# Two layers of Fourier mixing and sliding-window attention: preset far scores, a later weight split, a norm that starts sooner, and a fixed order of the last rows

## The chip, the core and the metric

The kernel runs on one core of a Trainium2 chip. A core has five engines that run their own instruction streams in order: TensorE (PE: matmuls, with weight loads shown apart as PEld), VectorE (DVE), ScalarE (ACT), GpSimd (POOL) and SyncE (SP), which here issues nearly all DMAs. SBUF is the working memory; matmuls write to PSUM, in banks of 512 float32 per partition. The metric is the device time of one execution in microseconds, lower is better. The time before is the median of three runs, 2053.36 us (2048.55 to 2053.51).

## The reference

Four sublayers are applied to one sequence of S = 2048 rows of D = 640: Fourier mixing, attention, Fourier mixing, attention, with the same weights both times.

```python
x = x + _A_ref(_layernorm(x), dft_seq_re, dft_seq_im, dft_hid_re, dft_hid_im)
x = x + _B_ref(_layernorm(x), wqkv, wo)
x = x + _A_ref(_layernorm(x), ...)
x = x + _B_ref(_layernorm(x), wqkv, wo)

def _A_ref(x, ...):          # real part of a two-dimensional DFT
    a, b = x @ hid_re.T, x @ hid_im.T
    return seq_re @ a - seq_im @ b

def _B_ref(x, wqkv, wo):     # H = 32 heads of 20, window W = 256
    q, k, v = split(x @ wqkv)
    scores = q @ k.T * 20 ** -0.5
    mask = (i - j >= 0) & (i - j < W)      # else -1e9
    return softmax(scores) @ v, heads joined, @ wo
```

## The kernel before, in words

Every float32 product is made of three fp16 matmuls: each operand is split into a high half and a remainder (`hi`, `lo`), and hi·hi, hi·lo and lo·hi are summed in PSUM. A split is a ScalarE cast (`hi`) and a subtraction on VectorE or GpSimd (`lo`).

`spectral` is the Fourier sublayer. `attention` is the other one; the change lies in it alone. It walks over steps G = 0 to 127 (`g` = 2G). A step is one tile of 128 query rows (`i`) and four heads; 16 steps make a block `b` of 256 rows (two tiles, eight groups of four heads), and even steps take the first tile of the block, odd ones the second. Block 0 is steps 0 to 15. A query tile sees three key tiles: its own, the one before and, two back, the far one, of which the causal window leaves the part above the diagonal.

In a step stand, on the engines named:

- `scores` (PE): near scores into the PSUM tiles `sq` (`near`), far scores into the first 256 columns of the PSUM tiles `sk` (`farq`). There are two of each, for two pairs of heads, and no second buffer: the next step writes the same tiles.
- `largest` (VectorE): L1175 copies the far scores over the masked triangle of the near ones, and L1177 takes the row maximum into `m`. The first two tiles (`i` < 2, steps 0 to 15) have no far tile; there the copy takes a constant tile `neg` in SBUF, spread over the heads.
- `by_key` and `probabilities` (PE, ScalarE L1231, GpSimd L1235 and L1237), 8 steps later: the scores once more, by key, with the maxima folded in as two more rows of the contraction, through an exponential into `ptq`, and the masks.
- `values` and `back`, 11 steps after the scores: the products with `v` (into `pf`, copied to `pvs` by ScalarE, L1263), two transposes with `idf`, a division on VectorE (`r` L1279, `o` L1280), and the split into `os` on GpSimd (L1282, L1283).
- one unit of filling work for PE (`run_unit`), 15 matmuls: projections of the next block to q and k (`pf<-early,big`, 128x256), to v (`pf<-big,early`, 128x320), or output products (`pf<-bo,ot`, 128x320). A unit is ready when its step has come and what it needs is done, and the one with the smallest due step goes first.
- one to three steps of slow work (`slow_step`): the norm of the rows that a later block projects (`rows_norm`: statistics L139, aggregates, eight small instructions L148 to L152, `lny` L166, and a split whose GpSimd half is `rx` L178), and, when none is left, idle work: in the first layer the split of the output weights.

That split is `split_wo`: five chunks of `wo`, each a load into `wst`, a ScalarE instruction (L1013) and a VectorE instruction (L1014) into `bo`. The first layer alone does it, from step 0 on. Output products need it (`"wo"` in a unit's needs).

The rows of blocks 2 and later are loaded from DRAM and normalised two blocks ahead. Those of block 2 are wanted at step 0, those of block 3 at step 6; a new norm was allowed only 4 `g` after the last had ended, and started 4 `g` behind its load.

At the end of a layer the last two tiles have no later work to hide behind. Their output products are made in three parts, for the 128-column groups 0 to 2, 3 and 4 of `os`, as soon as the last block's head groups give them: PE transposes `os` (`turned`), VectorE copies to `ot` (L1046), and the products are summed in the banks of `sq` and `sk` that are free by then. The three parts were units (`last_out`) in the order of their due steps.

`in_line` and `issue_after` keep the order in which the code is written on an engine; where they are not used, a list scheduler of the framework may place an instruction of VectorE or ScalarE a little earlier or later.

## Time and profile before

| | us |
|---|---|
| median of 3 runs | 2053.36 (2048.55 to 2053.51) |
| profiled execution | 2055.41 |
| its span, first to last instruction | 2053.7 |
| busy in the span: PE, DVE, POOL, ACT | 1986.1, 1568.6, 1475.1, 1112.4 |
| steps 0 to 15, first copy to that of step 16: layer one, layer two | 59.1, 58.4 |
| first copies of the layers | 557.7, 1568.1 |

The first attention starts with the copy at 557.7 us and the second with that at 1568.1 us. A row of the timeline has the start, the duration, the engine, the line, the operation with what it writes and reads, the number of merged instructions, and in brackets how long the engine had idled and for whom. Times of `pf` matmuls with the same operands can be compared with one another. "PEclk" in the windows view is the share of TensorE's clock that was granted in that stretch.

### The profile page before, as it was taken

To read this page: it belongs to the slowest core of one execution; us is meant where nothing else is said; L and a number is where in the kernel's file an instruction comes from. 1 tells how busy PE (TensorE), PEld (TensorE's weight loads), DVE (VectorE), ACT (ScalarE), POOL (GpSimd) and SP (SyncE) were. 2 spreads that over 40 slices of the span, in tenths; PEclk is the share of its full clock that TensorE was granted. 3 is DMA by queue.
4 is the path that set the end of the run, shared out by engine and by line. 5 is a ranking of instruction groups with operands and counts; after the bars stand their busy time and mean duration, and the time that the engine had idled before them with its cause. 6 is when DMAs were issued, how large, how long until landed. Compare 5 with 4: busy or idle time off the path is not lost.

```text
span 2053.7 us, 55762 instructions
## 1 busy us (share of the span) xinstructions
PE 1986.1 (97%) x21881; PEld 1449.5 (71%) x21881; DVE 1568.6 (76%) x3261; ACT 1112.4 (54%) x1959; POOL 1475.1 (72%) x2168
## 2 busy tenths in 40 slices
PE   6999999999989999999999999999999999999998
PEld 4777777776767777777667777777676677777765
DVE  8888778768588888777648778787776788886673
ACT  5544555534247777666644444444332576766665
POOL 5777788877457788776657778777783587777754
PEclk9999999999999999999999999999999999999999
DMA  7556566566544544434645455454744454443232
GB/s 274 178 197 203 174 209 226 179 242 215 148 111 102 126 125 112 105 93 103 166 132 177 153 184 178 151 172 145 284 161 129 88 129 118 120 121 95 72 85 74
DMA packets 280508, 311.10 MB, mean 151 GB/s; under 512 B 107572, under 2 KB 214836, under 8 KB 271156
## 3 DMA queue, kind: packets, MB, share of 16 engines
q1 hardware_dynamic: 279668, 306.88, 50.0%
q8 instruction: 171, 2.80, 0.6%
q14 instruction: 93, 0.76, 0.1%
q10 hardware_dynamic: 576, 0.66, 0.1%
HBM read 201.72 MB, written 83.46 MB: 139 GB/s over the span
## 4 chain that ended last, share of the span: by engine, by line
PE 69%; DVE 14%; issue 5%; POOL 4%; DMA 4%; ACT 3%; SPq 0%; DVEq 0%; POOLq 0%; ACTq 0%
PE pf L126 32%; PE y L126 11%; PE x L126 11%; PE z L126 7%; PE sk L126 5%; DVE cc L558 3%; PE sq L126 3%; DVE sq L1175 2%; DVE m L1177 2%; ACT ptq L1231 2%; DMA res<-accd 2%; DVE lnt L151 1%; POOL cs L548 1%; DVE res L581 1%; DVE lnst L139 1%
## 5 line engine op out<-in xcount | busy, mean ns | idle before, releaser
L126 PEld LDWEIGHTS <-cc 128*128 128x128 f16 x5376 | 524.4, 98 | 213.1 <-issue 13.4
L1231 ACT ACTIVATE ptq<-sk,shift,alpha 128x768 f32<-128x768 f32 (+2 forms) x512 | 472.5, 945 | 122.9 <-PE sk L126 70.7
L126 PEld LDWEIGHTS <-big 128*128 128x128 f16 x4320 | 415.1, 99 | 131.0 <-issue 25.0
L1177 DVE TENSOR_REDUCE m<-sq 128x2 f32<-128x512 f32 (+1 forms) x512 | 345.6, 675 | 19.4 <-POOL os L1282 0.5
L126 PE MATMUL pf<-early,big 128*128 128x256 f16 x2400 | 295.1, 277 | 0.1
L555 ACT ACTIVATE cc<-cs 128x512 f16<-128x512 f32 x256 | 153.7, 625 | 260.3 <-POOL cs L548 149.8
L126 PE MATMUL y<-zc,cc 128*128 128x320 f16 x1728 | 262.8, 299 | 3.2 <-DVE pf L581 3.2
L1235 POOL TENSOR_SCALAR_AFFINE_SELECT ptq<-ptq 128x512 f32<-128x512 f32 x224 | 142.7, 637 | 167.7 <-ACT ptq L1231 165.1
L558 DVE SCALAR_TENSOR_TENSOR cc<-cs,cc 128x512 f16<-128x512 f32 x256 | 248.1, 978 | 7.6 <-ACT cc L555 7.5
L1175 DVE COPY_PREDICATED sq<-mask,sk 128x256 f32<-128x256 int32 x448 | 189.5, 423 | 53.4 <-PE sq L126 51.6
L558 DVE SCALAR_TENSOR_TENSOR cc<-cq,cc 128x512 f16<-128x512 f32 x192 | 205.8, 1073 | 0.1
L126 PE MATMUL pf<-ptq,v 128*32 128x128 f32 (+1 forms) x3840 | 183.6, 329 | 3.1 <-DVE x L956 2.6
L126 PE MATMUL z<-zc,cc 128*128 128x320 f16 x1152 | 177.7, 299 | 5.4 <-DVE res L581 4.4
L1237 POOL TENSOR_SCALAR_AFFINE_SELECT ptq<-ptq 128x512 f32<-128x512 f32 x256 | 166.1, 649 | 19.6 <-ACT ptq L1231 19.4
L126 PE MATMUL x<-zc,cc 128*128 128x320 f16 x1152 | 177.7, 299 | 0.0
L387 ACT ACTIVATE qf<-pf 128x256 f32<-128x256 f32 x160 | 61.2, 383 | 166.1 <-PE pf L126 132.8
L126 PEld LDWEIGHTS pf<-ptq,v 128*32 128x32 f32 x3840 | 110.7, 110 | 45.5 <-DVE x L956 3.9
L126 PE MATMUL pf<-big,early 128*128 128x320 f16 x960 | 141.4, 300 | 0.0
L547 POOL TENSOR_TENSOR cs<-cq 128x512 f32<-128x512 f32 x64 | 86.8, 1357 | 68.3 <-DVE cc L558 67.7
L126 PEld LDWEIGHTS <-qs 62*128 62x128 f16 x2688 | 90.3, 94 | 59.1 <-issue 55.8
L126 PE MATMUL pf<-bo,ot 128*128 128x320 f16 x840 | 123.8, 300 | 0.8 <-DVE x L956 0.8
L126 PE MATMUL x<-big 128*128 128x320 f16 x825 | 122.3, 299 | 2.0 <-DVE big L447 2.0
(144 smaller groups left out, 3484.3 us busy)
## 6 DMA issues: line engine op xcount, KB each, us to landing
cq<-in_cmat_dram SPq DMA_DIRECT2D x64, 1024.0 KB
accd<-res SPq DMA_DIRECT2D x96, 320.0 KB
res<-accd SPq DMA_DIRECT2D x96, 320.0 KB
x<-x2d SPq DMA_DIRECT2D x64, 320.0 KB
qkd<-early SPq DMA_DIRECT2D x160, 128.0 KB
ks<-qkd SPq DMA_DIRECT2D x108, 160.0 KB
qs<-qkd SPq DMA_DIRECT2D x84, 160.0 KB
x2d<-res SPq DMA_DIRECT2D x32, 320.0 KB
```

The lines of the kernel that those rows point to most:

```text
L126: i = getattr(nc.tensor, what)(*args, **kw)
L139: nc.vector.bn_stats(st[:, h], x[:, h * 320:(h + 1) * 320])
L151: ts(u, g, g, h, op0=OP.mult, op1=OP.mult)
L387: nc.scalar.activation(f, pf[:, :QB], AF.Copy, scale=down)
L547: g.tensor_tensor(s1, a21, a22, op=OP.add)
L555: nc.scalar.activation(cc[m][:, 0], f, AF.Copy, scale=C_UP)
L558: nc.vector.scalar_tensor_tensor(cc[m][:, 1], f, C_UP, cc[m][:, 0], op0=OP.mult, op1=OP.subtract)
L1175: marks["dve"] = nc.vector.copy_predicated(near[pi][:, :, 0], mask[:, None, :].to_broadcast([P, 2, P]), far).ins
L1177: marks["dve"] = nc.vector.tensor_reduce(TOP[n][:, pi, :, k], near[pi][:, :, :1 + (i >= 1)], axis=AX.XY, op=OP.max).ins
L1231: marks["act"] = nc.scalar.activation(o[:, pi], tps[pi][:, :, first:], AF.Sigmoid, bias=shift, scale=alpha[:, 0:1]).ins
L1235: nc.gpsimd.affine_select(out=q[:, :, a0], in_=q[:, :, a0], pattern=[[0, 4], [-1, P]], base=0, channel_multiplier=1, compare_op=OP.is_gt, ...
L1237: ins = nc.gpsimd.affine_select(out=q[:, :, a0 + 2], in_=q[:, :, a0 + 2], pattern=[[0, 4], [1, P]], base=0, channel_multiplier=-1, compare ...
```

## The change

1. Far scores preset: `neg` is gone. At the start of each attention VectorE sets the far columns of both `sk` tiles to NEG, in PSUM, and for `i` < 2 the copy reads them there as it reads far scores later.
2. The weight split is queued at `g` = 34 (step 17, in block 1) in place of step 0, with two slow steps in place of three between chunks. Output tiles of block 0 wait for it, also their load and transposition.
3. Rows of block 3: the next rows' load may be issued as soon as a norm has ended, and the norm starts 8 `g` after the last one's end at the earliest.
4. In the second layer the last two tiles follow one generator, `last_rows`, that goes part by part and tile by tile, and `turn_rows` issues the transposes of a part as soon as its `os` is there. The first layer keeps `last_out`.
5. The last head group's `os` split is on ScalarE and VectorE in place of GpSimd, in both layers, and the second tile's last copy to `ot` in the second layer is on ScalarE.

```diff
+            for f in farq:
+                nc.vector.memset(f, NEG)
...
-                far = farq[pi] if i >= 2 else neg[:, None, :].to_broadcast([P, 2, P])
-                    marks["dve"] = nc.vector.copy_predicated(near[pi][:, :, 0], mask[:, None, :].to_broadcast([P, 2, P]), far).ins
+                    marks["dve"] = nc.vector.copy_predicated(near[pi][:, :, 0], mask[:, None, :].to_broadcast([P, 2, P]), farq[pi]).ins
...
+WO_STEP = 34
-            if layer == 0:
-                idle.append(split_wo())
+                if layer == 0 and g == WO_STEP:
+                    idle.append(split_wo())
-                    for _ in range(3):
+                    for _ in range(2):
-                        need = [(i - 2, 2)] if i > 1 else []
+                        need = [(i - 2, 2)] if i > 1 else ["wo"] * (layer == 0)
...
-            wanted, x2s, normed_at = [], [], [-FREE_STEPS]
+            wanted, x2s, normed_at = [], [], [-2 * FREE_STEPS]
-                if wanted and x2s and g >= x2s[0] + 4 * (g > 0):
+                if wanted and x2s and g >= max(x2s[0] + 4 * (g > 0), normed_at[0] + 2 * FREE_STEPS):
-                if wanted and not slow and not x2s and g >= normed_at[0] + FREE_STEPS:
+                if wanted and not slow and not x2s and g > normed_at[0]:
...
-                nc.gpsimd.tensor_copy(hi, o)
-                nc.gpsimd.tensor_tensor(lo, o, hi, op=OP.subtract)
+                if last and k == NP // 2 - 1:
+                    nc.scalar.activation(hi, o, AF.Copy)
+                    nc.vector.tensor_tensor(lo, o, hi, op=OP.subtract)
+                else:
+                    nc.gpsimd.tensor_copy(hi, o)
+                    nc.gpsimd.tensor_tensor(lo, o, hi, op=OP.subtract)
...
+            def last_rows(tiles):
+                for i in tiles:
+                    while (i - 2, 2) not in done:
+                        yield 0
+                    x3 = keep.tile([P, D], F32, tag="res1", name="x3", bufs=2)
+                    load(x3, x2_d[i])
...
+                for k in range(3):
+                    for i in tiles:
+                        while (i, k) not in turned_at or turned_at[i, k] >= now[0] or i % 2 and now[0] < NG + 2 * KEY_LAG \
+                                or k == 1 and len(parts) < 3:
+                            yield 0
+                        ot, acc, x3 = OT[i]
+                        d0, d1, at = parts[k]
+                        for n in range(2):
+                            yield from out_products(ot, acc[n], n, d0, d1)
...
+            def turn_rows():
+                for k, (d0, d1, at) in enumerate(parts if final else ()):
+                    for i in (S // P - 2, S // P - 1):
+                        if (i, k) not in turned_at and i in OT and at < now[0]:
+                            for _ in turned(i, d0, d1, i % 2 and d1 == ND):
+                                pass
+                            turned_at[i, k] = now[0]
```

How the rows of an engine's stream move is shown at three places, all on VectorE. (Line numbers of the changed kernel are higher: L1175 became L1218, L1177 L1220, L1014 L1050, L166 L165, L1046 L1085, L1279 and L1280 L1322 and L1323.) First, the end of step 1 and step 2 of the first layer's attention; before:

```order
L1175 COPY_PREDICATED sq_6969<-mask,neg 128x256
L1177 TENSOR_REDUCE m<-sq_6969 128x2
L1014 SCALAR_TENSOR_TENSOR bo_67<-wst,wsc,bo_66 128x640
L1175 COPY_PREDICATED sq_6968<-mask,neg 128x256
L1014 SCALAR_TENSOR_TENSOR bo_67<-wst,wsc,bo_66 128x640
L1177 TENSOR_REDUCE m<-sq_6968 128x2
L1175 COPY_PREDICATED sq_6969<-mask,neg 128x256
L1177 TENSOR_REDUCE m<-sq_6969 128x2
L139 BN_STATS lnst<-x_7003 128x6 x2
```

and with the change:

```order
L1218 COPY_PREDICATED sq_6967<-mask,sk_6969 128x256
L1220 TENSOR_REDUCE m<-sq_6967 128x2
L1218 COPY_PREDICATED sq_6966<-mask,sk_6968 128x256
L1220 TENSOR_REDUCE m<-sq_6966 128x2
L1218 COPY_PREDICATED sq_6967<-mask,sk_6969 128x256
L1220 TENSOR_REDUCE m<-sq_6967 128x2
L138 BN_STATS lnst<-x_7003 128x6 x2
```

Both splits of `bo` are gone from between the copies, and the copies read `sk`; the two MEMSETs that fill it stand ahead of the layer's first copy.

Second, the end of the norm of block 2's rows, and the copies of step 6; before:

```order
L166 TENSOR_SCALAR lny<-x_7003,lnmv,lnt 128x640
L152 TENSOR_SCALAR lnt<-lnt 128x1
L151 TENSOR_SCALAR lnt<-lnt 128x1
L152 TENSOR_SCALAR lnt<-lnt 128x1
L166 TENSOR_SCALAR lny<-x_7004,lnmv,lnt 128x640
L1175 COPY_PREDICATED sq_6968<-mask,neg 128x256
L1177 TENSOR_REDUCE m<-sq_6968 128x2
L1175 COPY_PREDICATED sq_6969<-mask,neg 128x256
L1177 TENSOR_REDUCE m<-sq_6969 128x2
```

and with the change:

```order
L165 TENSOR_SCALAR lny<-x_7003,lnmv,lnt 128x640
L151 TENSOR_SCALAR lnt<-lnt 128x1
L150 TENSOR_SCALAR lnt<-lnt 128x1
L151 TENSOR_SCALAR lnt<-lnt 128x1
L1218 COPY_PREDICATED sq_6966<-mask,sk_6968 128x256
L165 TENSOR_SCALAR lny<-x_7004,lnmv,lnt 128x640
L1220 TENSOR_REDUCE m<-sq_6966 128x2
L1218 COPY_PREDICATED sq_6967<-mask,sk_6969 128x256
L1220 TENSOR_REDUCE m<-sq_6967 128x2
```

The first copy of the step now stands ahead of the second `lny`; its maximum still follows that `lny`.

Third, the end of the second layer; before:

```order
L1046 COPY ot<-pf 128x2x384
L1279 RECIPROCAL r<-pf 128x8
L1280 TENSOR_TENSOR o<-pf,r 128x160
L1046 COPY ot<-pf 128x2x384
L1046 COPY ot<-pf 128x2x128
L1279 RECIPROCAL r<-pf 128x8
L1280 TENSOR_TENSOR o<-pf,r 128x160
L1046 COPY ot<-pf 128x2x128 x3
```

and with the change:

```order
L1085 COPY ot<-pf 128x2x384 x2
L1322 RECIPROCAL r<-pf 128x8
L1323 TENSOR_TENSOR o<-pf,r 128x160
L1085 COPY ot<-pf 128x2x128 x2
L1322 RECIPROCAL r<-pf 128x8
L1323 TENSOR_TENSOR o<-pf,r 128x160
L1328 TENSOR_TENSOR os<-o,os 128x2x80
L1085 COPY ot<-pf 128x2x128
```

Both tiles' copies of the first part now stand together, and the copies of the second part lie ahead of the last division; the last split (L1328) is VectorE's, and one copy of the last part has left for ScalarE. On PE the transposes of the first tile's first part now precede the last but one group of key products, the products of the second part follow the last `pvs` transposes, and the last products are the third part's 12 as before.

The five weight splits now stand on VectorE behind the 42nd, 44th, 48th, 68th and 70th copy of the first layer, where they stood behind the 4th, 5th, 20th, 40th and 44th; ScalarE's halves stand correspondingly. In fifteen places of blocks 1 to 4 of the first layer PE's filling unit is another than before, an output product for a projection or the other way, and each is 15 matmuls as before; no other engine but SP has more or fewer instructions than the five points say.

More of the change, by code (lines that the diff above doesn't have):

```diff
@@ L88, in body @@
     mask = pers.tile([P, P], I32, name="mask")
-    neg = pers.tile([P, P], F32, name="neg")
     shift = pers.tile([P, 1], F32, name="shift")
@@ L97, in constants @@
         nc.gpsimd.memset(mask, 1)
-        nc.gpsimd.memset(neg, NEG)
         nc.gpsimd.memset(shift, SHIFT)
@@ L933, in last_out @@
                         yield from next_layer(i, x3)
+            def last_rows(tiles):
[4 more added lines that the diff above has]
+                    load(x3, x2_d[i])
+                    OT[i] = (sb.tile([P, 2, ND, P], F16, tag="ot", name="ot", bufs=2),
+                             [t[:, 4 * P:] for t in kst] if i % 2 else qst, x3)
+                for k in range(3):
[7 more added lines that the diff above has]
+                            yield from out_products(ot, acc[n], n, d0, d1)
+                            if d1 == ND:
+                                cs = slice(n * 320, (n + 1) * 320)
+                                nc.vector.scalar_tensor_tensor(x3[:, cs], acc[n][:, :320], beta, x3[:, cs], op0=OP.mult, op1=OP.add)
+                                if final:
+                                    nc.scalar.dma_start(dst[i][:, cs], x3[:, cs])
+                        if d1 == ND and not final:
+                            yield from next_layer(i, x3)
+            def turn_rows():
[5 more added lines that the diff above has]
+                            turned_at[i, k] = now[0]
             def out_products(ot, o, n, d0, d1):
@@ L1045, in turned @@
                             yield 56
-                nc.vector.tensor_copy(OT[i][0][:, :, d0:d1], pt)
+                if act:
+                    nc.scalar.activation(OT[i][0][:, :, d0:d1], pt, AF.Copy)
+                else:
+                    nc.vector.tensor_copy(OT[i][0][:, :, d0:d1], pt)
                 yield 56
             OS, OT, X2, done = {}, {}, {}, {}
-            lastd, outs = [0], []
+            parts, turned_at, outs = [], {}, []
             credit = [0.0]
@@ L1099, in run_unit @@
                         n += 1 if ns else 15
+                    elif ns == 0:
+                        unit[0].at = now[0] + 1
+                        fill.append(unit[0])
+                        unit[0] = None
+                        continue
                     else:
@@ L1281, in back @@
                                                        r.unsqueeze(2).to_broadcast([P, 8, DH]), op=OP.mult).ins
-                nc.gpsimd.tensor_copy(hi, o)
-                nc.gpsimd.tensor_tensor(lo, o, hi, op=OP.subtract)
                 last = b == NBQ - 1
+                if last and k == NP // 2 - 1:
+                    nc.scalar.activation(hi, o, AF.Copy)
+                    nc.vector.tensor_tensor(lo, o, hi, op=OP.subtract)
+                else:
+                    nc.gpsimd.tensor_copy(hi, o)
+                    nc.gpsimd.tensor_tensor(lo, o, hi, op=OP.subtract)
                 d1 = (k + 1) * 4 * DH // P
                 if last and d1 > k * 4 * DH // P and (d1 > 2 or k > LAST_FROM):
-                    tiles = (2 * b, 2 * b + 1)
-                    for m, ts in enumerate([tiles] if d1 == ND else [tiles[:1], tiles[1:]]):
-                        step0 = max(now[0] + LAST_STEPS[0], NG + 2 * KEY_LAG if m else LAST_STEPS[1] if d1 < ND else 0)
-                        fill.append(Unit(step0, last_out(ts, lastd[0], d1), "last", NS + 2 * d1 + m, [(i - 2, 2) for i in ts]))
-                    lastd[0] = d1
+                    tiles, d0 = (2 * b, 2 * b + 1), parts[-1][1] if parts else 0
+                    if final and not parts:
+                        fill.append(Unit(now[0], last_rows(tiles), "last", NS, [(2 * b - 2, 2)]))
+                    parts.append((d0, d1, now[0]))
+                    if not final:
+                        for m, ts in enumerate([tiles] if d1 == ND else [tiles[:1], tiles[1:]]):
+                            step0 = max(now[0] + LAST_STEPS[0], NG + 2 * KEY_LAG if m else LAST_STEPS[1] if d1 < ND else 0)
+                            fill.append(Unit(step0, last_out(ts, d0, d1), "last", NS + 2 * d1 + m, [(i - 2, 2) for i in ts]))
                 elif k == NP // 2 - 1 and not last:
@@ L1425, in attention @@
                 run_fill(1600)
+                turn_rows()
                 for _ in range(8):
```

3 lines of the change are left out of this document (2 added, 1 removed).

## The prediction

> **What bounds the kernel now.** I read the page's busy line and chain first, then the waits of TensorE in the first 120 us of each attention block, then the granted clock by stretches.
>
> ```profile
> PE 1986.1 (97%) x21881; PEld 1449.5 (71%) x21881; DVE 1568.6 (76%) x3261; ACT 1112.4 (54%) x1959; POOL 1475.1 (72%) x2168
> PE 69%; DVE 14%; issue 5%; POOL 4%; DMA 4%; ACT 3%; SPq 0%; DVEq 0%; POOLq 0%; ACTq 0%
> PE sq L126 <- DVE m L1177: 7.0, 10, 1.5
> PE sq L126 <- DVE m L1177: 4.7, 6, 1.5
> ```
>
> PE is the bound: busy 97% of the span, 69% of the chain. Time can come only from where it stops. The two wait rows (total, times, longest) are of 553 to 680 us, the first attention block's start, and of 1564 to 1690 us, the second's: PE waits 7.0 and 4.7 us for `m`, VectorE's maxima, since `sq` cannot be overwritten before L1177 has reduced it. These waits cost more than themselves. A row of the windows view gives the stretch, its length, then busy time of PE, PEld, DVE, ACT, POOL, then the granted clock:
>
> ```profile
> 580.00:584.00 4.00, 1.47 (x17) 0.95 (x15) 3.43 (x5) 0.61 (x3) 3.53 (x5) 0.99 0.49 129
> 584.00:588.00 4.00, 4.00 (x24) 2.87 (x22) 1.74 (x4) 1.05 (x3) 2.40 (x5) 0.58 0.76 154
> 608.00:616.00 8.00, 6.21 (x71) 3.97 (x68) 6.73 (x23) 2.90 (x7) 4.12 (x10) 0.79 0.16 45
> 616.00:1588.00 972.00, 954.52 (x10531) 697.26 (x10528) 745.61 (x1536) 520.11 (x913) 704.53 (x1032) 1.00 0.50 147
> 1592.00:1596.00 4.00, 4.00 (x21) 2.76 (x21) 2.13 (x4) 1.24 (x3) 1.69 (x2) 0.50 0.60 139
> 1620.00:1624.00 4.00, 3.55 (x36) 2.41 (x36) 3.75 (x12) 1.20 (x3) 2.32 (x5) 0.70 0.24 70
> ```
>
> The clock falls to about half behind four stalls, two in each block, and nowhere in the 972 us between. The first stall of each block comes with its cause:
>
> ```profile
> L1175 DVE COPY_PREDICATED sq<-mask,sk x448: 406/420/430, 616.8 to 2014.1; 128x256 f32<-128x256 int32 x150
> L1175 DVE COPY_PREDICATED sq<-mask,neg x64: 406/432/1626, 557.7 to 1622.5; 128x256 f32<-128x256 int32 x64
> 573.16 0.91 DVE L1175 COPY_PREDICATED sq<-mask,neg 128x256 f32<-128x256 int32 x1
> 579.45 1.67 POOL L178 TENSOR_TENSOR rx<-lny,rx 128x640 f16<-128x640 f32 x1
> 579.78 1.63 DVE L1175 COPY_PREDICATED sq<-mask,neg 128x256 f32<-128x256 int32 x1
> 581.85 0.84 DVE L1175 COPY_PREDICATED sq<-mask,neg 128x256 f32<-128x256 int32 x1
> 581.99 0.21 PE L126 MATMUL sq<-ks 62*128 62x128 f16 x1 [1.53 <-DVE m L1177]
> 583.20 0.38 PE L126 MATMUL sq<-ks 62*128 62x128 f16 x7 [1.00 <-DVE m L1177]
> 575.05 3.45 PE L126 MATMUL pf<-early,big 128*128 128x256 f16 x30
> 583.67 5.12 PE L126 MATMUL pf<-early,big 128*128 128x256 f16 x30
> 1592.15 6.14 PE L126 MATMUL pf<-early,big 128*128 128x256 f16 x30
> ```
>
> The copy that reads `neg` from SBUF takes up to 1.63 us; the same copy from PSUM (`sk`) never more than 0.43 in 448. The 1.63 us one starts inside POOL's 1.67 us instruction and ends 0.3 us behind it: it was held. PE then waits 1.53 and 1.00 us, and the next 30 matmuls take 5.12 us instead of 3.45 (6.14 in the second layer).
>
> [...]
>
> **The change part by part.**
>
> (1) Far scores preset. Two MEMSETs of 128x256 in PSUM per layer come, and the 64 copies read PSUM. No row shows such a MEMSET; the nearest is the same-size copy, 0.42 us, so 0 to 0.9 us for two. They stand in this idle time of VectorE, in the first layer and the second:
>
> ```profile
> 557.71 0.43 DVE L1175 COPY_PREDICATED sq<-mask,neg 128x256 f32<-128x256 int32 x1 [4.04 <-PE sq L126]
> 1568.14 0.43 DVE L1175 COPY_PREDICATED sq<-mask,neg 128x256 f32<-128x256 int32 x1 [1.76 <-PE sq L126]
> ```
>
> 4.04 and 1.76 us: nothing. If the cover were gone, up to 0.9 us a layer. At the first stall the copies of 0.91, 1.63 and 0.84 become 0.42 each: VectorE is 2.1 us earlier. VectorE worked without a break there (3.43 of 4 us), so the waits of 2.53 us shrink by 2.1 to about 0.4. Two layers: **-4.2**. Bounds: 0 (the engine is late for other reasons) to -5.1 (all of both).
>
> (2) The clock behind it. With 0.4 us of waiting left I take the half-clock stretch as gone: 5.12-3.45 = 1.67 and 6.14-3.45 = 2.69, together **-4.4**. Bounds: 0, and -5.1: half of the half-clock time, which is 0.42x4x2 = 3.4 us in the first layer and, by the longer matmul row, twice that in the second. VectorE has room for the faster PE: it was busy 1.74 of 4 us from 584 to 588. The nearest row for a stall that did not cost clock is the pair of 1.23 and 0.58 us under (3), and the clock that is lost by 617 us (0.05x64 = 3.2 us, by the row of the third rival) is that of the two drops, 1.7 each.
>
> [...]
>
> (3) The weight split leaves the first steps.
>
> ```profile
> 564.25 0.88 DVE L1014 SCALAR_TENSOR_TENSOR bo<-wst,wsc,bo 128x640 f16<-128x640 f32 x1 [1.81 <-ACT bo L1013]
> 565.89 0.88 DVE L1014 SCALAR_TENSOR_TENSOR bo<-wst,wsc,bo 128x640 f16<-128x640 f32 x1 [0.41 <-ACT bo L1013]
> 567.16 0.21 PE L126 MATMUL sq<-ks 62*128 62x128 f16 x1 [1.23 <-DVE m L1177]
> 567.96 0.38 PE L126 MATMUL sq<-ks 62*128 62x128 f16 x7 [0.58 <-DVE m L1177]
> 628.36 1.41 DVE L1014 SCALAR_TENSOR_TENSOR bo<-wst,wsc,bo 128x640 f16<-128x640 f32 x1 [0.47 <-ACT bo L1013]
> 628.64 0.44 PE L126 MATMUL pf<-idf,pvs 128*128 128x128 f32 x2 [0.48 <-ACT pvs L1263]
> ```
>
> Two splits stand in front of a copy, which waits for ScalarE's half (1.81 and 0.41 us idle), and PE pays 1.23+0.58: **-1.8**. All five now stand in the second and third block of queries. Their price there is seen at the fourth: 1.41 us on VectorE, and PE waits 0.48 for a `pvs` that ScalarE makes behind its half of the split. Two stand there already, five will: three more at 0.3 to 0.5 is **+1.0** (0 if slack takes them, +3 if each costs a microsecond). Queued behind a split on VectorE is the next copy, on ScalarE `pvs` and `ptq`; PE waits for both. The early loads leave the SP queue as well; no wait of PE in these rows is for what stood behind them. The output products that need the split change places with value products, 15 matmuls of the same form 128x320 each: 0.
>
> (4) The second norm's rows sooner. The second stall:
>
> ```profile
> 603.58 0.43 DVE L1175 COPY_PREDICATED sq<-mask,neg 128x256 f32<-128x256 int32 x1 [0.66 <-PE sq L126]
> 605.73 0.88 DVE L139 BATCH_NORM_STATS2 lnst<-x 128x6 f32<-128x320 f32 x2
> 609.82 0.21 PE L126 MATMUL sq<-ks 62*128 62x128 f16 x1 [1.05 <-DVE m L1177]
> 610.77 0.38 PE L126 MATMUL sq<-ks 62*128 62x128 f16 x7 [0.74 <-DVE m L1177]
> 612.43 2.89 PE L126 MATMUL pf<-early,big 128*128 128x256 f16 x15
> ```
>
> The first tile's statistics now stand four copies earlier, so that the 0.66 us in which VectorE idled is used. VectorE gains about 1.1 us (the 0.88 of two statistics and an aggregate) and what other copies above 0.42 us give here, 1.5 in all as an estimate; PE gets a new wait of some 0.4 us two steps earlier, since VectorE then comes to that copy 1.1-0.66 later. VectorE stays nearly saturated here (6.73 of 8 us), so what the clock gives back (2.89 for 15 matmuls against 3.45 for 30: 1.2, and more in the groups beside them) is partly waited away: I take VectorE's own 1.5 us per layer, **-3.0**. Bounds: 0, and 1.79 of waits plus 1.7 of clock (half of 0.21x8x2) per layer, -7.0.
>
> (5) The last rows. A fixed order puts a tile's transposes ahead of key products, which cover the copy to `ot` that PE waited for, and 12 products behind the last `pvs` transpose.
>
> ```profile
> PE sk L126 <- DVE ot L1046: 1.4, 2, 0.9
> PE sq L126 <- DVE ot L1046: 1.3, 3, 0.7
> 2043.28 0.38 ACT L1263 ACTIVATE pvs<-pf 128x256 f32<-128x256 f32 x1 [4.95 <-PE pf L126]
> 2045.53 0.38 PE L126 MATMUL pf<-idf,pvs 128*128 128x128 f32 x2
> ```
>
> PE waits 2.7 us for these copies; the last `pvs` is ready at 2043.66 and its transpose comes 1.87 us later. Following the new order with these durations, waits of 0.5 (first copy), 0.5 (`pvs` behind the last two `ptq`), 0.5 (last split and copy) and small ones of 0.3 remain, 1.8: **-0.9** (0 to -2.7). The last head group's split on ScalarE and VectorE in POOL's place is inside the third 0.5; in the first layer, where the old order stays, the transposes that read it stand behind other products: 0.
>
> Sum: -4.2-4.4-1.8+1.0-3.0-0.9 = -13.3. The profiled execution took 2055.41 us (span 2053.7), 2.05 above the median of the runs, 2053.36; it would become 2042.1, the median **2040**.
>
> **The rivals.** *The clock does not follow the stalls* (12%). For it: the waits are short beside the half-clock stretches, and a stall of 1.8 us in all cost no clock at 567. Against it: the clock was half only behind the two stalls of each block. Then (2) goes, and about 0.5 of (4) per layer: 2040+4.4+1.0 = 2045.5.
>
> *VectorE is the bound anyway* (10%): in the first 64 us it is busy 47.7, and late from the norm rather than from the held copies. Then only (3), (5) and a third of (1) stand, -3: 2050.
>
> *The moved split stalls PE* (7%, the slower side). `bo` reads two SBUF operands as the `neg` copy does, and the 1.41 us at 628.36 shows it stretched. POOL is busier where it goes:
>
> ```profile
> 553.00:617.00 64.00, 55.39 (x546) 39.33 (x544) 47.66 (x121) 25.69 (x55) 32.27 (x81) 0.95 0.53 130
> 617.00:671.00 54.00, 52.54 (x785) 39.27 (x783) 47.63 (x110) 39.39 (x69) 42.67 (x89) 1.00 0.44 108
> ```
>
> 79% against 50%, and VectorE 88%. If each of the five is held 1.6 us, PE waits some 1.5 us, and from two such waits within one clock stretch it pays 1.7 more: 5x3.2 = 16, in place of the +1.0: 2055.
>
> **How the numbers follow.** Forecast 71% (its own range 2035 to 2045.5, from the bounds of (2) and (4)), rivals 12, 10 and 7%. The range 2034 to 2049 takes the forecast, the first rival and part of the second; the low end is the bounds of (4) and (5) in part and a run as low as 2048.55. A measurement of this kernel tells 0.3%, 6.2 us, from no change: faster is 2047.2 and below. The forecast and the first rival lie there, 0.82 with what they leave; within 0.3% the second, 0.11; slower 0.07.
>
> **What would show it.** No copy over 0.45 us; granted clock 1.00 in every stretch of both blocks' starts; PE's waits for `m` down from 7.0 and 4.7 us to about 2.5 and 1.5; `bo` at 630 to 680 us with waits below 0.6 us each behind it; the last 12 products about 0.9 us sooner after the last values. Half-clock stretches that remain behind waits under 1 us would prove (2) wrong; waits for `m` as long as before without a held copy, (1).

## The result

The changed kernel takes 2038.28 us (median of 4 runs, 2037.36 to 2039.46); the kernel before, on the same chip, 2051.32 us (4 runs, 2048.55 to 2053.51). The ratio is 0.9936, with a 95% interval of 0.9923 to 0.9949: 13.0 us faster. The prediction was 2040, in a range of 2034 to 2049.

### The profile after

Of the page of the changed kernel, the busy line and the chain by engine:

```profile
PE 1980.0 (97%) x21881; PEld 1445.3 (71%) x21881; DVE 1565.3 (77%) x3266; ACT 1112.0 (55%) x1962; POOL 1466.2 (72%) x2163
PE 65%; DVE 16%; issue 6%; POOL 5%; DMA 4%; ACT 4%; SPq 0%; DVEq 0%; POOLq 0%; ACTq 0%
```

PE has the same instructions and is still the bound at 97%, but is busy 6.1 us less. These are matmuls that ran at half clock before and run at full clock now: the profile before holds five half-clock windows of 3.41 us, this one holds one. Then the groups of the copies (ns: least, median, longest) and of the new MEMSETs (busy us, mean ns of one, idle before):

```profile
L1218 DVE COPY_PREDICATED sq<-mask,sk x512: 406/421/430, 555.9 to 1997.5; 128x256 f32<-128x256 int32 x171
L861 DVE MEMSET sk<- 128x256 f32 x4 | 1.1, 272 | 0.3
```

And TensorE's waits for `m` from 553 to 680 us and from 1564 to 1690 us (total, times, longest):

```profile
PE sq L125 <- DVE m L1220: 0.7, 3, 0.3
PE sq L125 <- DVE m L1220: 0.5, 2, 0.3
```

No copy takes over 0.43 us, where one in each layer took 1.63. The waits for `m` fall from 7.0 to 0.7 us and from 4.7 to 0.5. The windows view (PE, PEld, DVE, ACT, POOL busy, then the granted clock) of the first steps of both layers:

```profile
556.00:607.00 51.00, 50.18 (x532) 36.79 (x530) 41.67 (x118) 22.32 (x51) 28.32 (x66) 1.00 0.48 113
1560.00:1611.00 51.00, 50.23 (x531) 36.68 (x529) 41.67 (x118) 22.37 (x50) 28.51 (x66) 1.00 0.45 109
```

The granted clock is 1.00 in both. By the starts of VectorE's copies the spans of the two profiled executions divide as follows (each entry is rounded by itself):

| stretch | before, us | after, us |
|---|---|---|
| start to the first copy, layer one | 557.7 | 555.9 |
| block 0, layer one (32 copies) | 59.1 | 50.4 |
| blocks 1 to 4, layer one | 227.5 | 228.5 |
| from there to the last copy | 172.3 | 172.4 |
| last copy to the first of layer two | 551.5 | 552.5 |
| block 0, layer two | 58.4 | 50.4 |
| blocks 1 to 7, to the last copy | 387.5 | 387.5 |
| last copy to the end | 39.6 | 38.4 |
| span | 2053.7 | 2036.0 |

The spans differ by 17.7 us and the medians by 13.0, since the profiled execution of the kernel before took 2055.41 us, 4.1 above the median of its runs here, and that of the changed kernel 2037.70, 0.6 below. Why the former was so long can be read against the trace of the run with the tail alone (below), in which both blocks 0 are as in the kernel before. The profile before has five windows of half clock there and the other three (58.4 against 56.0 us in layer two). It also waits 2.11 us for a DMA at 555 us, and 1.23 and 0.58 us at 566 us at a weight split, where the other waits 0.56 us in all.

Two places became longer. In blocks 1 to 4 of the first layer PE now waits longer for the sums of output products; the waits of the kernel before from 680 to 910 us:

```profile
PE pf L126 <- DVE x L956: 1.6, 4, 0.8
```

and of the changed one there:

```profile
PE pf L125 <- DVE x L992: 2.9, 6, 0.8
PE pf L125 <- ACT qf L386: 0.9, 2, 0.5
```

And one half-clock stretch stands behind a wait of 1.82 us at the end of the first layer. Both kernels have this wait, but in the profile of the kernel before no half clock followed it: there it falls into two windows of the clock, with 1.51 and 0.31 us. Here it falls into one, which is idle for 1.92 us in all. In the timeline, and in the windows before and behind its end:

```profile
1004.93 0.31 PE L125 MATMUL sk<-ks,qs 62*128 62x128 f16 x4 [1.82 <-ACT ptq L1274]
```

```profile
1002.50:1005.87 3.37, 1.45 (x29) 0.99 (x27) 3.30 (x7) 1.58 (x3) 2.16 (x5) 1.00 0.51 97
1005.87:1009.28 3.41, 3.41 (x42) 1.75 (x37) 2.38 (x5) 2.04 (x4) 1.81 (x5) 0.50 0.54 157
```

### The profile page after: what moved, and what is told of

Read it like the earlier page. It is cut to its first block, busy times and chain, and to the rows that moved or that the text cites. A ratio compares the mean times of both kernels' runs of the same rounds, so it can differ in the third digit from the quotient of the medians.

```text
span 2036.0 us, 55799 instructions
## 1 busy us (share of the span) xinstructions
PE 1980.0 (97%) x21881; PEld 1445.3 (71%) x21881; DVE 1565.3 (77%) x3266; ACT 1112.0 (55%) x1962; POOL 1466.2 (72%) x2163
## 4 chain that ended last, share of the span: by engine, by line
PE 65%; DVE 16%; issue 6%; POOL 5%; DMA 4%; ACT 4%; SPq 0%; DVEq 0%; POOLq 0%; ACTq 0%
PE pf L125 31%; PE y L125 10%; PE x L125 10%; PE z L125 7%; PE sk L125 5%; DVE cc L557 4%; PE sq L125 3%; DVE sq L1218 2%; ACT ptq L1274 2%; DMA res<-accd 2%; DVE m L1220 2%; DVE res L580 1%; DVE lnt L150 1%; POOL cs L547 1%; DVE lnst L138 1%
## 5 line engine op out<-in xcount | busy, mean ns | idle before, releaser
L1220 DVE TENSOR_REDUCE m<-sq 128x2 f32<-128x512 f32 (+1 forms) x512 | 345.6, 675 | 18.9
L125 PE MATMUL pf<-early,big 128*128 128x256 f16 x2400 | 288.1, 273 | 1.3 <-ACT qf L386 0.9
L1218 DVE COPY_PREDICATED sq<-mask,sk 128x256 f32<-128x256 int32 x512 | 216.5, 423 | 67.8 <-PE sq L125 64.7
L1280 POOL TENSOR_SCALAR_AFFINE_SELECT ptq<-ptq 128x512 f32<-128x512 f32 x256 | 164.1, 641 | 21.9 <-ACT ptq L1274 21.8
```

The lines of the kernel that those rows point to most:

```text
L125: i = getattr(nc.tensor, what)(*args, **kw)
L1218: marks["dve"] = nc.vector.copy_predicated(near[pi][:, :, 0], mask[:, None, :].to_broadcast([P, 2, P]), farq[pi]).ins
L1220: marks["dve"] = nc.vector.tensor_reduce(TOP[n][:, pi, :, k], near[pi][:, :, :1 + (i >= 1)], axis=AX.XY, op=OP.max).ins
L1280: ins = nc.gpsimd.affine_select(out=q[:, :, a0 + 2], in_=q[:, :, a0 + 2], pattern=[[0, 4], [1, P]], base=0, channel_multiplier=-1, compare ...
```

## The experiments

The theory is that the copy that reads `neg` from SBUF is held by a GpSimd instruction that reads SBUF, that PE waits for it, that the clock halves behind the wait, and that the norm's statistics make a second such stall. The rivals are that the clock does not follow the stalls, that VectorE is late from the norm anyway, and that the moved split stalls PE. The code edits below are excerpts; `...` marks what is left out.

### Each part alone on the kernel before

**The preset alone.** Edit: `neg` goes, and

```diff
+            for f in farq:
+                nc.vector.memset(f, NEG)
...
-    far = farq[pi] if i >= 2 else neg[:, None, :].to_broadcast([P, 2, P])
+    far = farq[pi]
```

> The kernel before with part 1 alone: the far columns of sk are preset in PSUM and the copies of block 0 read them; neg is gone. Theory (terms 1 and 2): no copy above 0.45 us, the waits of the first stall of each block (1.53 and 1.00 us) shrink to about 0.4 together, and the half-clock stretch behind them is gone; the second stall, behind the norm's statistics, stays with its waits (1.05 and 0.74) and its clock. Time -8.6 us. Rival 'the clock does not follow the stalls': the waits go, the half-clock stretch stays, -4.2. Rival 'VectorE is late from the norm anyway': held copies go, PE's waits stay above 1.5 us, -1.4.

Measured: 2041.06 us against 2050.18, ratio 0.9954 (0.9942 to 0.9966): -9.1 us. The theory's number (-8.6) lies in this interval, the two rivals' (-4.2, -1.4) don't. The second stall did not stay as it was: it came sooner and in one piece. In the timeline of this run (layer one, then layer two):

```profile
598.52 0.88 DVE L137 BATCH_NORM_STATS2 lnst<-x 128x6 f32<-128x320 f32 x2
599.56 0.83 DVE L137 BATCH_NORM_STATS2 lnst<-x 128x6 f32<-128x320 f32 x2
601.37 0.32 DVE L1279 TENSOR_TENSOR o<-pf,r 128x160 f32<-128x160 f32 x1
601.74 0.66 PE L124 MATMUL sk<-ks 62*128 62x128 f16 x4 [2.64 <-DVE o L1279]
1607.84 0.65 PE L124 MATMUL sk<-ks 62*128 62x128 f16 x8 [1.44 <-ACT ptq L1230]
```

Both tiles' statistics and the small instructions behind them fill VectorE from 598.52 to 601.1, and the division `o` and the step's copies come behind. PE waits 2.64 us in one piece; a half-clock stretch follows at 601.5.

**The norm's pacing alone.**

```diff
-    wanted, x2s, normed_at = [], [], [-FREE_STEPS]
+    wanted, x2s, normed_at = [], [], [-2 * FREE_STEPS]
...
-    if wanted and x2s and g >= x2s[0] + 4 * (g > 0):
+    if wanted and x2s and g >= max(x2s[0] + 4 * (g > 0), normed_at[0] + 2 * FREE_STEPS):
...
-    if wanted and not slow and not x2s and g >= normed_at[0] + FREE_STEPS:
+    if wanted and not slow and not x2s and g > normed_at[0]:
```

> The kernel before with part 3 alone: the next rows' load is issued as soon as a norm has ended and the norm begins 8 g behind it. Theory (term 4 as a gain of its own): the second stall of each block goes or shrinks below 0.5 us of waiting, its half-clock stretch with it, the first stall stays: -3.0, with -7 as the bound. Rival: the statistics only move to where VectorE is still late from the held copies, so that the second stall moves up and stays: 0 within 1 us. Then the gain of parts 1 and 3 together is more than their sum.

Measured: 2049.70 us, ratio 0.9997 (0.9988 to 1.0005): -0.5 us, which can't be told from nothing. That is the rival's number. In the second layer the waits for `m` stand as before at the first stall (1.54 and 1.00 us) and are 0.46 and 0.74 at the second, 0.6 us shorter; in the first layer 1.26 us stand at the first stall in place of 2.53, and 2.26 and 0.73 us at 566 us in place of 1.23 and 0.58, where a weight split waits for its load:

```profile
562.95 1.63 ACT L1013 ACTIVATE bo<-wst,wsc 128x640 f16<-128x640 f32 x2 [2.42 <-DMA wst<-in_wo_dram]
563.81 0.89 DVE L1014 SCALAR_TENSOR_TENSOR bo<-wst,wsc,bo 128x640 f16<-128x640 f32 x1 [3.18 <-ACT bo L1013]
566.37 0.21 PE L126 MATMUL sq<-ks 62*128 62x128 f16 x1 [2.26 <-DVE m L1177]
```

Block 0 is only a little shorter in the one layer, 57.0 us, and no shorter than with the tail alone in the other, 56.5 against 56.0.

**The weight split alone.**

```diff
+WO_STEP = 34
...
-                        need = [(i - 2, 2)] if i > 1 else []
+                        need = [(i - 2, 2)] if i > 1 else ["wo"] * (layer == 0)
...
-            if layer == 0:
-                idle.append(split_wo())
...
+                if layer == 0 and g == WO_STEP:
+                    idle.append(split_wo())
...
-                    for _ in range(3):
+                    for _ in range(2):
```

> The kernel before with part 2 alone: the split of the output weights starts at g = 34 of the first layer, one slow step less between chunks, and output tiles of block 0 wait for it. Theory (term 3): the waits of 1.23 and 0.58 us at 566 to 568 us are gone, the two stalls of each block stay; blocks 1 and 2 give back about 1.0: -0.8. In the trace of the changed kernel the second block of queries is 1.0 us shorter and the third 1.3 us longer, with PE waiting three times 0.81 us for an output sum that stands behind a norm: so what is given back should be seen at output products, not at the splits. Also open: the wait of 2.11 us for the first stacks at 555 us is gone in the changed kernel; if the early loads of the output weights cause it, it is gone here too and the time is another 1.8 us shorter, -2.6; if it comes and goes with the DMAs, it is there or not in any of the four.

Measured: 2049.78 us, ratio 0.9994 (0.9986 to 1.0003): -0.4 us. In its trace blocks 1 to 4 of the first layer have the lengths that they have in the changed kernel (52.7, 58.8, 58.5, 58.5 us), so what was given back there is this part's doing. The wait for the first operands of the scores at 555 us (2.11 us in the profile of the kernel before) is absent here, absent with the preset alone and with the tail alone, and 0.51 us with the norm alone: it comes and goes. Over all runs the first copy starts between 555.4 and 558.8 us, so the 1.8 us before it in the table are not shown to be the change's.

**The tail alone**: the changed kernel with the other three parts taken back.

> The kernel before with parts 4 and 5 alone: the fixed order of the last rows in the second layer, and the last head group's split on ScalarE and VectorE in both layers. Theory (term 5): the last 40 us lose 0.9 to 1.1 us, all else stays: -0.9. Rival: the copies to ot were hidden by other waits and the end does not move, 0.

Measured: 2050.51 us, ratio 1.0000 (0.9991 to 1.0009). Inside this interval of 1.8 us either way the time can't tell; the trace can. From the last copy to the end it takes 38.4 us, as the changed kernel does, against 39.6: -1.2. The waits for `ot` of the changed kernel in that stretch are 0.8 us in three, where the kernel before had 2.7 in five:

```profile
PE sq L125 <- DVE ot L1085: 0.5, 2, 0.3
PE pf L125 <- DVE ot L1085: 0.3, 1, 0.3
```

Alone the parts give -9.1, -0.5, -0.4 and +0.3: -9.7. Together they give -13.0. By the intervals above this difference could still be chance; the next runs ask directly which part works only beside another. They and the run of the changed kernel belong to different sets of runs, in which the kernel before had medians of 2050.30, 2051.04 and 2051.32 us, so differences of about 1 us between sets tell nothing.

### Each part taken back from the changed kernel

**Without the preset** (the copies of block 0 read `neg` in SBUF again, as in the kernel before).

> The changed kernel with part 1 taken back: the copies of block 0 read neg from SBUF again. If the parts add (preset alone -9.1 us against the kernel before), this is 2047.4. If the norm's new pacing gains only where the copies aren't held (alone it gave -0.5, and in the run with the preset alone PE still waited 2.64 and 1.44 us for the norm's statistics), the preset is worth more here than alone and this is about 2049, 0.3 to 1 us below the kernel before.

Measured: 2047.42 us, against 2050.30 before 0.9984 (0.9973 to 0.9996): 9.1 us above the changed kernel. Reckoned each from the kernel before in its own set (2.9 and 13.0 us), the difference is 10.2. So the preset is worth about the same alone and beside the rest.

**The old pacing of the norm** (the diff above, reversed).

> The changed kernel with part 3 taken back. Alone on the kernel before, part 3 gave -0.5 us. If it is worth as little here, 2038.8. If what it does is to spread the statistics that stand in one row ahead of a division (PE waited 2.64 and 1.44 us for it in the run with the preset alone), these waits are back here, with a half-clock window where the grid of windows has them in one piece: 2040.5 to 2042.

Measured: 2042.17 us, against 2051.04 before 0.9959 (0.9945 to 0.9973): 3.9 us above the changed kernel. All seven executions (2039.80 to 2045.03) lie above all four of the changed kernel. So this is the part that needs another: beside held copies its 0.5 us can't be told from nothing, without them it is worth 3.9. The wait is like the one of 1.44 us that the preset alone left in the second layer; here it stands in both layers, each time with a half-clock window behind it:

```profile
600.06 0.88 DVE L138 BATCH_NORM_STATS2 lnst<-x 128x6 f32<-128x320 f32 x2
601.09 0.83 DVE L138 BATCH_NORM_STATS2 lnst<-x 128x6 f32<-128x320 f32 x2
602.90 0.33 DVE L1323 TENSOR_TENSOR o<-pf,r 128x160 f32<-128x160 f32 x1
604.21 0.64 PE L125 MATMUL sk<-ks 62*128 62x128 f16 x8 [1.50 <-ACT ptq L1274]
```

**The old place of the weight split** (reversed as well).

> The changed kernel with part 2 taken back: the weight split from step 0 on, three slow steps between chunks. By term 3 it loses: the wait of 0.58 us of the run with the preset alone comes back at 565 us, with the splits' time on VectorE, +0.8 net. By the waits of the changed kernel (0.81 us three times and 0.46 twice between 680 and 910 us for output products behind a norm, 3.35 against 1.34 before) it gains 2.0 there and loses 1.0 in block 0: -1.0, 2037.3.

Measured: 2038.94 us (2037.11 to 2039.98), 0.7 above the changed kernel, less than the two medians can be told apart by. Its trace has block 0 at 51.2 us against 50.4, blocks 1 to 4 at 227.3 against 228.5. The part moved a cost, and gained nothing that can be measured.

**The split at g = 16.** Edit: `WO_STEP = 16`.

> The changed kernel with the weight split queued at g = 16 in place of 34. The splits then stand behind copies of steps 13 to 19, just behind the norm. The output products keep most of their new places, since they go by their own due steps once the split is done. By the waits of the changed kernel, of which none stands at a split and three of 0.81 us stand at output sums: within 1 us of the changed kernel, 2037.5 to 2039. If the splits were what cost in blocks 1 and 2, as term 3 had it, moving them changes the waits there.

Measured: 2038.40 us (2037.95 to 2040.28), as forecast. One of the three waits of 0.81 us is gone; a wait of 1.69 us at 594 us, with a half-clock stretch behind it, is new, and block 0 takes 53.0 us. Moving the splits moves the stalls and not the total.

**The fixed order of the last rows in the first layer too.**

```diff
-                for k, (d0, d1, at) in enumerate(parts if final else ()):
+                for k, (d0, d1, at) in enumerate(parts):
...
-                    if final and not parts:
+                    if not parts:
...
-                    if not final:
+                    if False:
```

> The changed kernel with the fixed order of the last rows in the first layer too. The last rows of the first layer have waits of PE of 1.82, 0.51, 0.84, 0.65, 0.77, 0.54, 0.39 and 0.80 us in the changed kernel; in the second layer part 4 removed 2.0 us of such waits and 1.1 us of time. So -1.1, 2037.2. Rival: in the first layer the next Fourier mixing waits for the norm of these rows, which come in another order, and the gain is lost behind it: 0 to +2.

Measured: 2041.39 us (2038.92 to 2043.11), 3.1 slower than the changed kernel. The gain is lost, as the rival had it, but the loss is more than its 2 us and has another cause than it named:

```profile
1040.95 1.27 POOL L546 TENSOR_TENSOR cs<-cq 128x512 f32<-128x512 f32 x1
1042.18 1.27 POOL L548 TENSOR_TENSOR cs<-cq 128x512 f32<-128x512 f32 x1
1043.40 1.27 POOL L547 TENSOR_TENSOR cs<-cs,cq 128x512 f32<-128x512 f32 x1
1044.75 1.26 POOL L549 TENSOR_TENSOR cs<-cq,cs 128x512 f32<-128x512 f32 x1
1045.96 0.32 POOL L1330 CAST os<-o 128x160 f16<-128x160 f32 x1
1046.33 0.23 PE L125 MATMUL pf<-idh,os 128*128 128x128 f16 x1 [1.75 <-POOL os L1330]
```

Four instructions of the next Fourier sublayer (`cs`) stand on GpSimd ahead of a split into `os`, and the transposes that the fixed order puts next wait for it, 1.75 us; a half-clock stretch follows at 1046.9.

### Who holds the copy

The kernel before, in which GpSimd writes zeros into the low half `rx` of the rows of blocks 2 to 7, in place of the subtraction that reads SBUF: the low half of those rows is left out of the computation.

```diff
-                    split(xs[:, 0], xs[:, 1], y, nc.gpsimd)
+                    nc.scalar.activation(xs[:, 0], y, AF.Copy)
+                    nc.gpsimd.memset(xs[:, 1], 0.0)
```

> The kernel before, with the low half of every split of the rows of blocks 2 to 7 (rx) written as zeros by GpSimd in place of a subtraction that reads SBUF: the high half alone is used, so a part of the computation is left out. neg stays in SBUF. It asks whether the copy is held by GpSimd's instruction. Theory: the copy of 1.63 us, which stood inside the 1.67 us subtraction, falls to 0.43 or to at most 0.9 (other GpSimd instructions still read SBUF there), and the waits of 1.53 and 1.00 us fall by about 1.2 together in each block; with about 1.3 us left in one window the half-clock window behind it goes: -2 to -5 us. Rival (the copy is slow there for another reason, its two SBUF inputs or the DMAs): the longest copy stays at 1.6 us and the time within 1 us of the kernel before.

```profile
576.51 0.63 POOL L1031 MEMSET rx<- 128x640 f16 x1
577.09 0.65 POOL L388 CAST early<-qf 128x256 f16<-128x256 f32 x1
577.41 0.61 DVE L1176 COPY_PREDICATED sq<-mask,neg 128x256 f32<-128x256 int32 x1
578.47 0.42 DVE L1176 COPY_PREDICATED sq<-mask,neg 128x256 f32<-128x256 int32 x1
578.60 0.21 PE L126 MATMUL sq<-ks 62*128 62x128 f16 x1 [1.06 <-DVE m L1178]
```

The copy of 1.63 us takes 0.61, and that of 0.84 behind it 0.42; the longest copy of this run takes 0.91. So the rival, which had 1.6 us still, is out. But this run doesn't put a copy beside an instruction that only writes: the copy starts 0.27 us behind the end of the MEMSET, beside the cast into `early`. What stands beside the MEMSET is the norm's `lny`, just ahead of the copy:

```profile
576.34 1.15 DVE L166 TENSOR_SCALAR lny<-x,lnmv,lnt 128x640 f32<-128x640 f32 x1
```

In the kernel before it took 0.61 us. So of the 1.02 us that the copy gained, 0.54 were lost just ahead of it, in both layers alike, and the waits of 1.53 and 1.00 us only become 1.06 and 0.58.

What holds the copies is shown best by the trace of the kernel before. Of the 64 copies that read `neg`, 17 take over 0.45 us. Each of these starts while a GpSimd instruction runs that reads SBUF and writes it (into `rx`, `early`, `ptq` or `os`), and ends 0.28 to 0.29 us behind that instruction's end. In the changed kernel, where the copy reads PSUM, one that lies inside the same subtraction takes its usual time:

```profile
575.19 1.68 POOL L177 TENSOR_TENSOR rx<-lny,rx 128x640 f16<-128x640 f32 x1
575.87 0.42 DVE L1218 COPY_PREDICATED sq<-mask,sk 128x256 f32<-128x256 int32 x1
```

So the copy was held by GpSimd's instruction, through its operand in SBUF. The time of the run was missed: 2050.91 us against 2051.04, ratio 1.0007 (0.9995 to 1.0020). In the trace blocks 0 are shorter, but blocks 2 to 4 of the first layer are 1.5 us longer than before (57.8, 58.6 and 59.0 us against 57.5, 58.1 and 58.3), with a wait of 1.38 us for an output sum. What causes that wait stays open.

### What a wait costs in clock

The changed kernel, with reductions of 0.82 us on VectorE, whose result nothing reads, ahead of one copy: in the first run 2 to 6 of them at five steps of each layer, in the second 3 and 4 in turn at twelve.

```diff
...
+                for _ in range({28: 2, 44: 3, 60: 4, 76: 5, 92: 6}.get(G, 0) if pi == 0 else 0):
+                    with in_line("dve"):
+                        marks["dve"] = nc.vector.tensor_reduce(jmax, junk[:, None, :].to_broadcast([P, 5, P]), axis=AX.XY, op=OP.max).ins
```

> The changed kernel with idle reductions on VectorE (128x640 from SBUF, into a tile that nothing reads) ahead of the first copy of steps 28, 44, 60, 76 and 92 of each layer: 2, 3, 4, 5 and 6 of them, about 1.4 to 4.1 us. It measures what a wait of PE costs in clock. Reading of the six traces so far: the clock is set in windows of 3.413 us on a fixed grid, and halves for one window when PE was idle for more than about 1.8 us of the one before; a wait of 1.5 us costs nothing more, one of 2 us costs up to 1.7 us more, unless the grid splits it in two halves below 1.8; one of over 3.6 us always does. Rival (a whole idle window is needed): only the longest doses halve the clock. Rival (what follows a stall by its kind of work, not by its length): no dose does, since these steps stand where the clock was never half. The time is no matter here.

> The changed kernel with 3 and 4 idle reductions in turn ahead of the first copy of the steps 20, 28, ... 108 of each layer, so that waits of PE of two lengths (1.85 and 2.7 us by the run before) fall 24 times on changing places of the grid of 3.413 us. Reading: the wait that has more than about 1.8 us in one window is followed by a half-clock window, the same wait split by the grid is not; so of the shorter ones less than half, of the longer ones about three quarters. A half-clock window costs 1.2 us, by the second block of the kernel before and of the run with the tail alone (58.4 against 56.0 us with three windows against one). Rival: the length of the wait alone decides, so that all of the longer ones and none or all of the shorter ones are followed by one.

They took 2077.34 and 2107.53 us, with one execution each. In the first, the two waits of 1.59 us were followed by no half-clock window; of two waits of 1.85 and 2.04 us the shorter was; all six of 2.70 us and more by one, the longest, 4.50 us, by two. The rival that has the clock follow the kind of work is out: it halves at steps where it had never been half. So is the one that asks for a whole idle window, with waits of 2.7 us behind which it halves. The second run shows that the length alone doesn't decide either. Two waits of the same 2.71 us in it, in the timeline, and then the windows of the grid around each:

```profile
848.06 0.63 PE L128 MATMUL sk<-ks,qs 62*128 62x128 f16 x4 [2.71 <-ACT ptq L1280]
849.55 2.82 PE L128 MATMUL pf<-ptq,v 128*32 128x256 f32 x32
1881.31 0.21 PE L128 MATMUL sk<-ks,qs 62*128 62x128 f16 x1 [2.71 <-ACT ptq L1280]
1882.72 1.51 PE L128 MATMUL pf<-ptq,v 128*32 128x256 f32 x32
```

```profile
845.89:849.31 3.42, 1.00 (x24) 0.74 (x23) 3.35 (x8) 1.24 (x2) 1.23 (x2) 1.00 0.76 220
849.31:852.72 3.41, 3.41 (x43) 1.93 (x39) 3.27 (x9) 2.09 (x4) 1.40 (x3) 0.50 0.90 190
1876.70:1880.10 3.40, 1.91 (x15) 1.25 (x13) 3.30 (x5) 0.62 (x1) 1.23 (x3) 1.00 0.21 65
1880.10:1883.50 3.40, 1.93 (x45) 1.41 (x48) 3.25 (x10) 2.13 (x3) 1.23 (x2) 1.00 0.78 196
```

The grid is the row of windows of 3.413 us in which the clock is set. In the trace of the kernel before, the half-clock stretches start at 583.95, 611.26, 1590.88 and 1621.60 us, 8, 287 and 9 times 3.413 us apart, and last 3.41, 3.41, 6.83 and 3.41 us. The first wait has 2.2 us in one window, which is idle for 2.4 us in all (PE busy 1.00 of 3.42), and the next window has clock 0.50: 32 matmuls take 2.82 us in place of 1.51. The second is cut by the grid into 1.5 and 1.2 us, neither window is idle for more than 1.53 us in all, and the clock stays. Of this run's ten waits of 2.4 us and more, six were followed by a half-clock stretch. The other four were cut so that no window was idle for more than 1.8 us. Of the twelve shorter ones (1.40 to 2.10 us) two were followed by one. PE's idle time, summed by windows over the fourteen traces (windows at full clock, the program's two ends left out), gives a narrower limit. None with under 1.6 us is followed by half clock, of those with 1.6 to 1.9 us some are, and of those above 1.9 all but one.

Such a window costs about 1.2 us here. The lengths of the blocks 0 in the traces, in us, with the number of half-clock windows in brackets, show it:

| kernel | layer one | layer two |
|---|---|---|
| before | 59.1 (2) | 58.4 (3) |
| tail alone | 57.8 (2) | 56.0 (1) |
| norm alone | 57.0 (1) | 56.5 (2) |
| split alone | 55.5 (1) | 56.6 (2) |
| without GpSimd's read | 55.0 (0) | 55.8 (2) |
| changed, without the preset | 55.0 (1) | 53.8 (0) |
| preset alone | 53.9 (1) | 51.2 (0) |
| changed, old norm | 52.1 (1) | 52.2 (1) |
| changed, split at g = 16 | 53.0 (1) | 50.4 (0) |
| changed, fixed order twice | 50.4 (0) | 51.1 (0) |
| changed, old split | 51.2 (0) | 50.4 (0) |
| changed | 50.4 (0) | 50.4 (0) |

In layer two the first two rows run the same instructions with the same waits: two windows more are 2.4 us. In the rows "split alone" and "changed, without the preset" both layers run the same instructions in block 0, and one window more is 1.1 and 1.2 us. Layer one of the kernels that split the weights from step 0 also differs by the waits at 566 us.

## Why the prediction was right, step by step

The measured time is 1.7 us under the forecast of 2040; the gain is 13.0 us (from 2051.32) against the 13.3 of the sum (from 2053.36). The terms:

| term | forecast | alone | taken back |
|---|---|---|---|
| (1)+(2) preset and clock behind it | -8.6 | -9.1 | -9.1 |
| (3) weight split | -0.8 | -0.4 | -0.7 |
| (4) norm's rows sooner | -3.0 | -0.5 | -3.9 |
| (5) last rows | -0.9 | +0.3 (trace -1.2) | not run |

**(1) and (2): the sum right, the division off.** The copies fell to 0.43 us, the MEMSETs took 0.27 us each in the idle time of VectorE, and the waits and the half clock went, as the mechanism had it. But (1) was too small and (2) too large. The second layer of the changed kernel without the preset has no half-clock window and is 3.4 us longer than with it: the held copies' waits alone cost 3.4 us a layer, 6.8 in both, where (1) had 4.2. (1) counted three held copies a layer, 2.1 us. In the trace of the kernel before nine and eight are held, by 3.5 and 3.2 us together, and some of them belong to the second stall. (1) also left 0.4 us of waiting a layer at the first stall; no wait above 0.3 was left. Of the 9.1 us about 2.3 remain for the clock, where (2) had 4.4. (2) priced the half clock by the slowest group, 1.67 and 2.69 us; a window costs 1.2. Its larger term was a double window, which of the four traces with half clock behind this stall (before, norm, split and tail alone) two have. That the two errors cancel is luck.

By the traces, more than 1.9 us of waiting in one window of 3.413 us was followed by half clock in all cases but one, and under 1.6 us in none. The 17 held copies each started beside a GpSimd instruction that reads SBUF, and ended 0.28 to 0.29 us behind it. No run shows the copy beside one that only writes, since none starts beside GpSimd's zero write.

**(3): too small to be measured, with the cost at another place.** The two waits of 1.23 and 0.58 us went. But they come and go: of the five other traces with the split at step 0, three (tail alone, preset alone, old split) have 0.56 to 0.58 us there, one has 1.23 in all and one 2.99. The +1.0 was put down to three more splits of `bo` in blocks 1 and 2, at 0.3 to 0.5 us each; the trace shows no wait above 0.3 us at a split there. What costs is what the prediction put at 0: the output products that change places. Their sum `x` on VectorE now comes behind an `lny`, and PE waits 0.81 us in three places, of which the timeline of the changed kernel has one here:

```profile
829.00 0.97 DVE L165 TENSOR_SCALAR lny<-x,lnmv,lnt 128x640 f32<-128x640 f32 x1
829.89 0.54 DVE L992 SCALAR_TENSOR_TENSOR x<-pf,beta,x 128x320 f32<-128x320 f32 x1
830.49 1.51 PE L125 MATMUL pf<-ptq,v 128*32 128x256 f32 x32 [0.81 <-DVE x L992]
```

**(4): the right size for a reason that needs (1).** Its 3.0 us went by what VectorE gains; measured were 3.9 beside the preset and 0.5 without. Each layer's block 0 is 1.7 to 1.8 us longer with the old pacing, with one half-clock window in it. The prediction added the terms as if they stood apart. The -3.0 is right only because the preset is in the change too.

**(5)** was right by the traces, though its time alone can't be told from nothing: 0.8 us of waits for `ot` in place of 2.7, and a tail 1.2 us shorter.

**The rivals.** That the clock does not follow the stalls is refuted by the runs with added waits; what spoke for it, the stall of 1.8 us in all at 567 us without a loss of clock, was cut by the grid into 0.96 and 0.86 us. That VectorE is the bound anyway had a true core, the norm's row of statistics, but it was worth 3.9 us, and the change removes it. That the moved split stalls PE for 16 us is refuted: no wait of that kind is in the trace.

No run beat the changed kernel. Those with the split at step 0 or at g = 16 (2038.94 and 2038.40) stand level with it.

## What to carry to other kernels

Where TensorE is the bound, count its waits by windows of the clock and not by their sum: here no window with under 1.6 us of idle time was followed by half clock, and each half-clock window cost about 1.2 us on top of the waits ahead of it. An instruction that takes four times its usual time (here 1.63 us against 0.42) is worth more than its excess when a buffer without a double hangs on it; look at what the neighbour engine reads at that moment; here the copy, up to 1.63 us with `neg` in SBUF, took 0.43 us at most once that operand was in PSUM. Test edits that relieve the same engine together and apart: the norm's pacing was worth 3.9 us once the held copies were gone, and nothing that could be measured before.

## What the runs showed of the hardware that was not expected

TensorE's clock was set in windows of 3.413 us on a grid; the half-clock stretches of the kernel before start 8, 287 and 9 times that apart. Whether a stall of 1.8 to 2.7 us cost clock went by where the grid cut it, and that differed between executions. The two waits of 2.71 us above are one example. Another is the stall of 1.06 and 0.74 us near the end of block 0 in layer two: in the trace of the kernel before, 1.81 us of idle time fell into one window, and the next had clock 0.50; in that with the tail alone 1.38 us did, and the next had 1.00. In the kernel before, with four stalls of 1.8 to 2.5 us in its blocks 0, the executions spread from 2046.4 to 2058.4 us; the changed kernel, with one wait of 1.8 us left, from 2037.4 to 2039.5. So one profiled execution can hold more or fewer half-clock windows than the median does: the one shown ahead of the prediction held five, another with the same stalls three. And in it, and in the run with the norm alone, two such windows followed directly on one another, where 0.55 and 0.58 us of the stall fell into the first of them. In other runs 0.52 and 0.63 us in a half-clock window were followed by full clock, so what decides behind a half-clock window stays open.

In the run without GpSimd's read, `lny` on VectorE took 1.15 us in both layers with the MEMSET of `rx` beside it, a GpSimd instruction that only writes; in the kernel before, with the subtraction there, it took 0.61. No run separates the cause.
